# Moving a low part to GpSimd, the last phi(q) forward, and the sixth modulation vector back, in an adaLN block with linear attention and a token-mixing MLP

## The chip, the cores and the metric

One core of a Trainium2 chip runs the kernel. The metric is the device time of one execution in microseconds (us). The core has a matrix engine (PE), a vector engine (VectorE, DVE in the rows), a scalar engine (ScalarE, ACT), a general engine (GpSimd, POOL) and a queue that issues transfers (SyncE, SP). Each of them works through its own list of instructions strictly in order, and waits for the others by semaphores.

## The reference

x has S = 2048 tokens of D = 448 channels, and c is one row that conditions the block. All is float32.

```
mod = (silu(c) @ w_mod) -> sa, ca, ga, sb, cb, gb      # six vectors of D
h = layernorm(x) * (1 + ca) + sa
q, k, v = h @ wqkv                                      # 16 heads of 28
pq, pk = phi(q), phi(k)        # phi(t) = (t + 1 if t > 0 else exp(t)) + 1e-6
kv, z = pk^T v, sum(pk)                                 # per head, over all tokens
o = (pq kv) / (pq z + 1e-6)
x = x + ga * (o @ wo)
h = layernorm(x) * (1 + cb) + sb
u = gelu(h^T @ w1 + b1)                                 # over the token axis, F = 1792
x = x + gb * (u @ w2 + b2)^T
```

The sixth vector of mod, gb, has the index 5 in the kernel.

## The kernel before

The tokens are cut into 16 tiles of 128 (t = 0..15). Every large product is done in the matrix engine's 32-bit rounded format with the operand split in two: a high part (name ending in h) that ScalarE rounds off, and a low part (ending in l), the rest, which is a subtraction. Three products, high x high, high x low and low x high, are added up in one PSUM bank. There are eight banks, and a bank can be given to a new product only when its old contents have been read.

The program is written out in order: the order of the calls in the source is the order in which each engine gets its instructions, and there is no scheduler behind it. Tiles in SBUF come from pools, so that an instruction can also wait for the last reader of a buffer that is used again.

**First stage (0 to about 27 us).** For each token tile, ScalarE makes the high part `hh` of the transposed x, and `a_split_low` makes the low part `hl` on the engine that the tuple `POOL_LOW` names: GpSimd for the tiles in it, VectorE for all others. `projects` multiplies them by the weights into the banks `kp`. Layer norm is applied afterwards: VectorE makes statistics (`a_stats_dve`: `st` on one tile, `mv` and `ve` on a pair), GpSimd raises them to a power (`mv` from `ve` and `roots`), VectorE writes them to `rowst` (`a_rows`), PE transposes that into the bank `rw` (`a_transpose`), ScalarE copies it to the last rows of `hl`, and one more product (L439) closes `kp`. Then ScalarE makes `ek` and `rk` of a closed `kp` (exp and relu) and VectorE makes `pk` of those. The products `cacc` (L550, L554) gather pk^T h.

**Attention and second norm (i = 0..20 of the loop over `NT + LAG`).** Iteration i transposes `pn` of token tile i (bank `tq`, L857), multiplies tile i-1 by the output weights (bank `op`), and runs the first MLP product of tile i-5 for the first four of 14 column groups f (banks `up0` to `up3`, L944 to L946 in `acc3`). The list `late` holds q projections left for this loop; iteration 5 does the last, tile 15. `a_phi_q(nq)` at an iteration's end makes `eq` and `rq` on ScalarE and `pq` on VectorE for all that are projected, but leaves the newest for the next iteration. VectorE has, per iteration, `pd`, `den`, `pn` (attention's division), `x` and `y` (residual and second norm), `ptl` and `pth` (low parts of the transposed tile) and `h2l`, the low part of the MLP's input of which `h2h` is the high part. From iteration 17 on PE also begins the groups 4 to 7 on the first tiles (list `early`, banks `up4` to `up7`).

**The sixth modulation vector.** `mod_part(5, k)`, k = 0..3, adds up four row blocks of w_mod, scaled by silu(c), in `acc5` on VectorE; `mod_add` folds its halves; `mod_high` and its returned function split it into `mh5` on ScalarE and VectorE; `mod_sum2` sums over partitions with one matmul by ones (bank `modp5`, L253); `mod_out` copies the bank to `mod5` on ScalarE (L203), which frees the bank. In the kernel before, the four parts stand in iterations 13 to 16, one each, and the rest in iteration 16. `mod5` is first needed behind the first MLP product, in `finish_u`.

**Second MLP stage (from about 203 us).** The rest of the first MLP product, and then the second one (`y`, L1167 to L1171) by a seven-product scheme.

Of the kernel before, what the change touches and what calls it, by code (L numbers as in the profile page):

```python
# [39 lines left out]
MOD_AT = {11: [(4, 0), (4, 1), (4, 2)], 13: [(4, 3), (4, None), (3, 0), (3, 1)]}  # L40
QS = {0: 3}
WARM = 6
POOL_LOW = (0, 1, 2)
PRE = 9
MID = 5
NSLOT, NTOK = 74, 27
# [5 lines left out]
def block_kernel(ctx: ExitStack, tc: tile.TileContext, x, xt, wqkv, wo, w1, b1, w2, c, wmod, wfirst, out):  # L52
# [26 lines left out]
    def bank(name):  # L79
        return psum.tile([P, 512], F32, name=name, tag="bank")  # L80
# [164 lines left out]
    def mod_split(j):  # L245
        mod_add(j)
        mod_high(j)()
# [125 lines left out]
    def a_stats_dve(ts):  # L373
        g, ve = a_group(ts)

        b6 = {}

        def first(i):
            b6[i] = small.tile([P, 6], F32, name=f"st{ts[i]}", tag="st")
            nc.vector.bn_stats(b6[i], X[ts[i]])  # L380

        def second(i):
            nc.vector.bn_aggr(mv[ts[i]][:, 0:2], b6[i])

        def end():
            nc.vector.tensor_scalar_add(ve, g[:, :, 1:2].to_broadcast([P, len(ts), 2]), EPS)
            a_pow(g, ve)
            groups[ts[0]] = g
        return first, second, end
# [3 lines left out]
    def a_rows(t):  # L393
        g, r = groups.pop(t)[:, :, 0:2], rowst[t // 2 % RING].rearrange("p (t b c) -> p t b c", t=2, b=2)
        nc.vector.tensor_copy(r[:, :, :, 0:2], g.unsqueeze(2).to_broadcast([P, 2, 2, 2]))

        def low():
            nc.vector.tensor_sub(r[:, :, 0, 2:4], g, r[:, :, 0, 0:2].bitcast(F32))
        return low
# [81 lines left out]
    def a_phi_q(keep=0):  # L481
        a_exp_q(keep)
        for t in sorted(eqs):
            pq[t] = phi_q(t)
# [9 lines left out]
    def a_high(t):  # L494
        xss[t] = (slot(f"xh{t}", 512, F32R), slot(f"xl{t}", 384, F32R))
        nc.scalar.activation(xss[t][0][:, :D], xn[t], AF.Copy)
# [127 lines left out]
    a_split_high(6)  # L624
    a_exp(0, kps[0])
    a_high(0)
    low = a_rows(2)
    low()
    a_pk(0, kps[0])
# [1 line left out]
    projects(in_turn(5)[:4], 1, "kp")  # L631
    a_transpose(2)
    projects(in_turn(5)[4:], 1, "kp")
    first45, second45, end45 = a_stats_dve((4, 5))
    first45(0)
    first45(1)
    second45(0)
    second45(1)
# [306 lines left out]
        nc.tensor.matmul(ps[:, :D], hi[:, sl], ml, start=False, stop=False)  # L945
        nc.tensor.matmul(ps[:, :D], lo[:, sl], mh, start=False, stop=last)  # L946

    def step(f0, t, accs, mh, ml):
        k, at = place[f0, t]
        hi, lo = parts[k]  # L950
        for i, ps in enumerate(accs):
            acc3(ps, hi, lo, slice(at + i * P, at + (i + 1) * P), mh, ml, t == 0, t == NT - 1)
        if place.get((f0, t + 1), (0, 0))[0] != k:
            del parts[k]

    a_q(late.pop(0))
# [25 lines left out]
    for i in range(NT + LAG):  # L982
        if i == NT - 4:
            load_mod(5)
        if NT - 3 <= i <= NT:
            mod_part(5, i - NT + 3)
        if i == NT:
            mod_split(5)
        if i % 2 == 0 and 0 < i <= NT:
            b_out_last(i - 2)  # L990
        if i < NT:
            b_transpose(i)
        if 0 <= i - 1 < NT:
            b_out(i - 1)
        nq = min(len(late), QS.get(i, 1))
        for _ in range(nq):
            a_q(late.pop(0))
        t = i - LAG
        if t >= 0:
            if t == 0:  # L1000
                accs = [bank(f"up{f}") for f in range(4)]
            if i > NT:
                if not early:
                    early = [bank(f"up{W1G[1][0] + f}") for f in range(W1G[1][1])]
                r = i - NT - 1
                step(W1G[1][0], r, early, H2h[r], H2l[r])
            step(0, t, accs, H2h[t], H2l[t])
        if i == NT:
            mp = mod_sum2(5)
            mod_out(5, mp)  # L1010
        if i < NT:
            b_high(i)
            if i % 2 == 0:
                b_beside(i)
        a_exp_q(nq)
        scale, res, norm1, norm2 = i + 1 < NT, 0 <= i - 2 < NT, 0 <= i - 3 < NT, 0 <= i - 4 < NT
        if res and i < NT + 1:
            b_res(i - 2)
        if scale:
            b_prod(i + 1)  # L1020
        if norm2:
            b_norm2(i - 4, i)
        if res:
            b_mean1(i - 2, i)
        if norm1:
            b_norm1_a(i - 3)
        if scale:
            b_sum(i + 1)
        if norm1:
            b_norm1_b(i - 3, i)  # L1030
        if scale:
            b_eps(i + 1)
        if i < NT:
            b_low(i)
        if norm1:
            b_mean2(i - 3, i)
        split_end()
        if scale:
            b_recip(i + 1)
        if i < NT:  # L1040
            b_low_last(i)
        if scale:
            b_scale(i + 1)
        if i == NT:
            b_res(i - 1)
        if norm2:
            b_low2(i - 4)
        if i == 1:
            low3()
        if i == 2:  # L1050
            mod_out(3, mod_sum2(3))
        if i == 0:
            for ch in range(4):
                wp_split(ch)
        a_phi_q(nq)
        load_to(max(14 + (i + 1) // 2, 12 + max(0, i - 6) + max(0, i - 14)))
        if res or norm1:
            b_rstd(i, 0 if res else 1, 2 if norm1 else 1)
        split_to(8 + max(0, i - 5))


# [312 lines left out]
```

## Time and profile before

| what | us |
|---|---|
| median of 3 runs | 435.1 (434.35 to 435.51) |
| the profiled execution | 434.17 |
| its span, first to last instruction | 432.5 |
| PE busy | 427.6 (99%) |
| VectorE busy | 364.3 (84%) |
| ScalarE busy | 278.4 (64%) |
| GpSimd busy | 120.6 (28%) |
| granted PE clock | 1.000 |

The 1.7 us between the span and the profiled execution lie around the program and hold no instruction of it. A PE that is busy 99% is not one at its peak: a matmul's row lasts 0.36 us, but the next one starts 0.20 us after it, so that a short wait shows as a larger distance between two starts, even where the rows overlap and PE counts as busy. In a row of the timeline stand the start, the time, the engine, the line, the operation and the tiles written and read; the square brackets tell how long the engine was idle before and what ended that.

### The profile page before, as it was taken

How to read it: one execution, taken by the hardware profiler on the slowest of the kernel's cores; microseconds unless marked ns; L12 is line 12 of the kernel's file. 1: busy time of each engine (PE TensorE's matmuls, PEld its weight loads, DVE VectorE, ACT ScalarE, POOL GpSimd, SP SyncE). 2: the span in 40 equal slices, each digit the busy share in tenths (PEclk: the TensorE clock that was granted, in tenths of full speed). 3: DMA queues.
4: the chain of work that ended last, by engine and by line, in shares of the span. 5: the costliest groups of instructions: out<-in, count | busy, mean ns of one | idle time of the engine just before them, and what ended most of it. 6: DMA issues, size and time to landing. Idle time of an engine off the chain costs nothing.

```text
span 432.5 us, 7208 instructions
## 1 busy us (share of the span) xinstructions
PE 427.6 (99%) x2331; PEld 395.5 (91%) x2331; DVE 364.3 (84%) x814; ACT 278.4 (64%) x595; POOL 120.6 (28%) x199
## 2 busy tenths in 40 slices
PE   8999999999999999999999999999999999999997
PEld 7888899999899989989999999999999999999996
DVE  4999997889899899996579695739798998898894
ACT  5889868657678799985855263537464664655550
POOL 4336444300026577775200000010113131132010
PEclk9999999999999999999999999999999999999999
DMA  8999996564200036345427461577469977885431
GB/s 280 385 316 201 241 262 148 119 196 171 86 1 0 26 74 149 73 107 116 145 85 240 145 212 50 167 205 207 85 186 213 227 161 150 216 181 119 85 46 40
DMA packets 63797, 66.14 MB, mean 153 GB/s; under 512 B 4816, under 2 KB 55312, under 8 KB 63760
## 3 DMA queue, kind: packets, MB, share of 16 engines
q1 hardware_dynamic: 54688, 50.90, 38.1%
q0 software_dynamic: 8784, 14.32, 20.7%
q10 hardware_dynamic: 288, 0.46, 0.4%
q8 instruction: 18, 0.29, 0.3%
q14 instruction: 19, 0.16, 0.1%
HBM read 46.30 MB, written 7.34 MB: 124 GB/s over the span
## 4 chain that ended last, share of the span: by engine, by line
PE 91%; DMA 4%; DVE 3%; ACT 1%; issue 0%; DVEq 0%
PE y L1170 19%; PE up L945 10%; PE up L944 10%; PE up L946 10%; PE y L1171 9%; PE cacc L550 7%; PE qp L432 7%; PE op L887 6%; PE kp L432 5%; DMA xt<-in_xt_dram 2%; DMA wr<-in_qkv_dram 2%; PE tq L857 1%; PE op L894 1%; PE qp L439 1%; PE kvb L812 1%; PE wp L962 1%
## 5 line engine op out<-in xcount | busy, mean ns | idle before, releaser
L945 PE MATMUL up<-h2l,ph 128*128 128x448 f32 x224 | 81.3, 363 | 0.0
L944 PE MATMUL up<-h2h,ph 128*128 128x448 f32 x224 | 81.2, 363 | 0.0
L946 PE MATMUL up<-h2h,pl 128*128 128x448 f32 x224 | 80.8, 361 | 0.0
L1125 POOL DMA_DIRECT2D a<-a x16 | 14.2, 972 | 136.7 <-DMA pr<-in_B_w_dram 75.5
L944 PEld LDWEIGHTS up<-h2h,ph 128*128 128x128 f32 x224 | 42.0, 188 | 3.2
L946 PEld LDWEIGHTS up<-h2h,pl 128*128 128x128 f32 x224 | 41.9, 187 | 3.0
L945 PEld LDWEIGHTS up<-h2l,ph 128*128 128x128 f32 x224 | 42.0, 188 | 2.6 <-DVE h2l L941 0.3
L84 DVE TENSOR_TENSOR pl<-pr,ph 128x512 fp32r<-128x512 f32 x46 | 30.6, 685 | 4.1 <-ACT ph L83 3.3
L1176 ACT ACTIVATE cc<-y 128x448 f32<-128x448 f32 x24 | 13.0, 546 | 26.8 <-PE y L1171 26.8
L83 ACT ACTIVATE ph<-pr 128x512 fp32r<-128x512 f32 x46 | 27.6, 624 | 0.8 <-PE up L946 0.5
L1089 DVE TENSOR_TENSOR u<-u,mod 128x448 f32<-128x448 f32 x14 | 8.7, 621 | 21.7 <-ACT u L1088 21.5
L1190 POOL DMA_DIRECT2D out_dram<-yt x14 | 12.8, 911 | 41.8 <-DVE yt L1181 32.5
L1088 ACT ACTIVATE u<-up,b 128x448 f32<-128x448 f32 x14 | 8.8, 625 | 24.1 <-PE up L946 23.5
L432 PE MATMUL kp<-wh,hh 128*128 128x448 f32 x64 | 23.7, 376 | 0.2 <-ACT rk L449 0.2
L550 PE MATMUL cacc<-pkh,xh 128*128 128x448 f32 x64 | 23.6, 369 | 0.0
L432 PE MATMUL qp<-wh,hh 128*128 128x448 f32 x64 | 23.5, 368 | 0.0
L837 POOL TENSOR_SCALAR den<-den 128x16 f32<-128x16 f32 x16 | 8.8, 550 | 44.7 <-DVE den L834 44.7
L550 PE MATMUL cacc<-pkl,xh 128*128 128x448 f32 x56 | 20.3, 362 | 0.0
L887 PE MATMUL op<-wph,pth 128*128 128x448 f32 x48 | 18.7, 390 | 0.0
L1131 DVE TENSOR_TENSOR a<-a,s 128x512 f32<-128x512 f32 (+1 forms) x32 | 18.4, 616 | 0.0
L83 ACT ACTIVATE s2h<-s 128x512 fp32r<-128x512 f32 (+1 forms) x16 | 8.3, 569 | 15.5 <-DVE s L1131 15.5
L1170 PE MATMUL y<-ub,a11h 128*128 128x448 f32 x56 | 18.2, 375 | 0.0
(235 smaller groups left out, 1379.0 us busy)
## 6 DMA issues: line engine op xcount, KB each, us to landing
pr<-in_B_w_dram SPq DMA_DIRECT2D x56, 256.0 KB, 2.9
a<-in_B_w_dram SPq DMA_DIRECT2D x32, 256.0 KB, 4.6
a<-in_B_w_dram SPq DMA_DIRECT2D x32, 192.0 KB, 4.4
xt<-in_xt_dram SPq DMA_DIRECT2D x16, 256.0 KB, 5.0
x<-in_A_x_dram SPq DMA_DIRECT2D x16, 224.0 KB, 5.0
wm<-in_B_wmod_dram SPq DMA_DIRECT2D x16, 196.0 KB, 5.0
out_dram<-x SPq DMA_DIRECT2D x14, 224.0 KB, 2.4
out_dram<-yt POOLq DMA_DIRECT2D x14, 224.0 KB, 5.3
```

The lines of the kernel that those rows point to most:

```text
L83: nc.scalar.activation(hi, full, AF.Copy)
L84: nc.vector.tensor_sub(lo, full, hi.bitcast(F32))
L432: nc.tensor.matmul(pps[t, j][:, :D], a[:, ch * P:(ch + 1) * P], w, start=first, stop=False)
L550: nc.tensor.matmul(cacc[ch][:, :D], a[:, s], b, start=(t == 0 and i == 0), stop=(t == NT - 1 and i == len(todo) - 1))
L887: nc.tensor.matmul(opb[t][:, :D], a, b, start=(ch == n == 0), stop=False)
L944: nc.tensor.matmul(ps[:, :D], hi[:, sl], mh, start=first, stop=False)
L945: nc.tensor.matmul(ps[:, :D], hi[:, sl], ml, start=False, stop=False)
L946: nc.tensor.matmul(ps[:, :D], lo[:, sl], mh, start=False, stop=last)
L1125: nc.gpsimd.dma_start(w, a, accum_op=ALU.add)
L1131: nc.vector.tensor_tensor(w, raw2[q, a][i], raw2[q, b][i], op=op)
L1170: nc.tensor.matmul(ps[:, :D], h[:, s], w, start=opens and r == 0, stop=False, skip_group_check=True)
L1171: nc.tensor.matmul(ps[:, :HD], l[:, s], wh, start=False, stop=closes and r == PAIRS - 1, skip_group_check=True)
```

## The change

Three things are done in the source.

1. Token tile 5 joins `POOL_LOW`, so that its low part `hl5` is made by GpSimd, and the statistics of the tiles 4 and 5 are begun earlier in the source: `st4` stands before `rowst` of the tiles 2 and 3.
2. `a_phi_q(nq if late else 0)`: in the iteration that has the last q projection, nothing is left for the next iteration.
3. The four `mod_part(5, k)` and `mod_add(5)` stand together at the end of iteration 16, the split of `acc5` in iteration 17, and the matmul `modp5` and the copy `mod5` at the end of iteration 17. `early` gets three banks first; the fourth, `up7`, is taken after `modp5`, and its first tile is multiplied there (`step` gets a `cut` for that).

```diff
-POOL_LOW = (0, 1, 2)
+POOL_LOW = (0, 1, 2, 5)
...
     a_exp(0, kps[0])
     a_high(0)
+    first45, second45, end45 = a_stats_dve((4, 5))
+    first45(0)
     low = a_rows(2)
     low()
     a_pk(0, kps[0])
...
     a_transpose(2)
     projects(in_turn(5)[4:], 1, "kp")
-    first45, second45, end45 = a_stats_dve((4, 5))
-    first45(0)
     first45(1)
...
-    def step(f0, t, accs, mh, ml):
+    def step(f0, t, accs, mh, ml, cut=(0, None)):
         k, at = place[f0, t]
         hi, lo = parts[k]
-        for i, ps in enumerate(accs):
+        for i, ps in list(enumerate(accs))[slice(*cut)]:
             acc3(ps, hi, lo, slice(at + i * P, at + (i + 1) * P), mh, ml, t == 0, t == NT - 1)
-        if place.get((f0, t + 1), (0, 0))[0] != k:
+        if cut[1] is None and place.get((f0, t + 1), (0, 0))[0] != k:
             del parts[k]
...
-        if NT - 3 <= i <= NT:
-            mod_part(5, i - NT + 3)
-        if i == NT:
-            mod_split(5)
...
-                    early = [bank(f"up{W1G[1][0] + f}") for f in range(W1G[1][1])]
+                    early = [bank(f"up{W1G[1][0] + f}") for f in range(W1G[1][1] - 1)]
                 r = i - NT - 1
-                step(W1G[1][0], r, early, H2h[r], H2l[r])
+                step(W1G[1][0], r, early, H2h[r], H2l[r], (0, None if r else 3))
             step(0, t, accs, H2h[t], H2l[t])
-        if i == NT:
-            mp = mod_sum2(5)
-            mod_out(5, mp)
...
+        if i == NT + 1:
+            low5 = mod_high(5)
         if res:
             b_mean1(i - 2, i)
...
+        if i == NT + 1:
+            low5()
         if scale:
             b_eps(i + 1)
...
-        a_phi_q(nq)
+        a_phi_q(nq if late else 0)
...
+        if i == NT:
+            for k in range(4):
+                mod_part(5, k)
+            mod_add(5)
+        if i == NT + 1:
+            mod_out(5, mod_sum2(5))
+            early.append(bank(f"up{W1G[1][0] + 3}"))
+            step(W1G[1][0], 0, early, H2h[0], H2l[0], (3, None))
```

What this does to the order on the engines is shown at three places. A row has the line, the operation and the tiles written and read (the number behind a tile's name is its buffer's), and the shape.

VectorE at 20 to 24 us, in the kernel before, from the variance of the tiles 2 and 3 on:

```order
L415 TENSOR_TENSOR hl4_332<-xt4_153,hh4_331 128x512
L492 TENSOR_SCALAR xn0_357<-x0_135,mv0_282 128x448
L415 TENSOR_TENSOR hl5_346<-xt5_159,hh5_345 128x512
L395 CAST rowst1_103<-mv2_337 128x4x2
L398 TENSOR_TENSOR rowst1_103<-mv2_337,rowst1_103 128x2x2
L454 SCALAR_TENSOR_TENSOR pk0_396<-ek0_387,rk0_388 128x448
L501 TENSOR_TENSOR xh0_391<-xn0_357,xh0_391 128x64
L502 TENSOR_TENSOR xl0_392<-xn0_357,xh0_391 128x384
L380 BN_STATS st4_415<-x4_161 128x6
L380 BN_STATS st5_417<-x5_165 128x6
```

The same place with the change:

```order
L415 TENSOR_TENSOR hl4_332<-xt4_153,hh4_331 128x512
L492 TENSOR_SCALAR xn0_357<-x0_135,mv0_282 128x448
L380 BN_STATS st4_396<-x4_161 128x6
L395 CAST rowst1_103<-mv2_337 128x4x2
L398 TENSOR_TENSOR rowst1_103<-mv2_337,rowst1_103 128x2x2
L454 SCALAR_TENSOR_TENSOR pk0_400<-ek0_387,rk0_388 128x448
L501 TENSOR_TENSOR xh0_391<-xn0_357,xh0_391 128x64
L502 TENSOR_TENSOR xl0_392<-xn0_357,xh0_391 128x384
L380 BN_STATS st5_417<-x5_165 128x6
```

`st4` has taken the place of `hl5`, which has left this engine; on GpSimd it stands between the powers `mv2` and `mv4`.

ScalarE at 139 to 148 us, in the kernel before, from the relu of tile 14 on:

```order
L462 ACTIVATE rq14_1937<-qp14_1831,mv14_989 128x448
L935 ACTIVATE y1_1867<-y1_1867,nb1_1944,rt4_1886 128x448
L938 ACTIVATE h2h1_1947<-y1_1867 128x448
L340 ACTIVATE sqa3_1953,vs5_1952<-x3_157,nm3_1950 128x448
L340 ACTIVATE sqb2_1965,vs5_1952<-y2_1955,ny2_1963 128x448
L865 ACTIVATE pth6_2009<-tq6_1981 128x384
L861 ACTIVATE pn7_2012<-pn6_1970 128x64
L461 ACTIVATE eq15_2014<-qp15_1903,mv14_989 128x448
L462 ACTIVATE rq15_2015<-qp15_1903,mv14_989 128x448
```

The same place with the change:

```order
L462 ACTIVATE rq14_1937<-qp14_1831,mv14_989 128x448
L935 ACTIVATE y1_1867<-y1_1867,nb1_1944,rt4_1886 128x448
L938 ACTIVATE h2h1_1947<-y1_1867 128x448
L340 ACTIVATE sqa3_1953,vs5_1952<-x3_157,nm3_1950 128x448
L340 ACTIVATE sqb2_1965,vs5_1952<-y2_1955,ny2_1963 128x448
L461 ACTIVATE eq15_1973<-qp15_1903,mv14_989 128x448
L462 ACTIVATE rq15_1974<-qp15_1903,mv14_989 128x448
L865 ACTIVATE pth6_2015<-tq6_1987 128x384
L861 ACTIVATE pn7_2018<-pn6_1970 128x64
```

`eq15` and `rq15` have moved ahead of the copy of the transposed tile 6; on VectorE `pq15` moves likewise, from behind `h2l2` to directly behind `pq14`.

VectorE from the end of iteration 16 on, with the change (in the kernel before, the four `acc5` rows stand one each in iterations 13 to 16, and the fold and `mh5` ahead of x14):

```order
L903 SCALAR_TENSOR_TENSOR x15_932,sm15_2782<-op15_2736,x15_932 128x448
L941 TENSOR_TENSOR h2l12_2766<-y12_2711,h2h12_2765 128x448
L230 TENSOR_SCALAR acc5_2793<-wm5_0_2434,sc_194 112x448
L232 SCALAR_TENSOR_TENSOR acc5_2793<-wm5_1_2436,sc_194,acc5_2793 112x448
L232 SCALAR_TENSOR_TENSOR acc5_2793<-wm5_2_2438,sc_194,acc5_2793 112x448
L232 SCALAR_TENSOR_TENSOR acc5_2793<-wm5_3_2440,sc_194,acc5_2793 112x448
L237 TENSOR_TENSOR acc5_2793<-acc5_2793 48x448
L84 TENSOR_TENSOR pl18_2800<-pr18_2274,ph18_2799 128x512
L913 SCALAR_TENSOR_TENSOR y14_2840<-x14_867,nm14_2768,mod4_1477 128x448
L917 SCALAR_TENSOR_TENSOR y14_2840,sy14_2842<-y14_2840,rt16_2791,mod3_1737 128x448
L243 TENSOR_TENSOR mh5_2833<-acc5_2793,mh5_2833 64x448
L941 TENSOR_TENSOR h2l13_2831<-y13_2773,h2h13_2830 128x448
```

Nine rows lie between x15 and `mh5`, of which five make `acc5`.

PE around the matmul `modp5`, in the kernel before:

```order
L946 MATMUL up3_1918<-h2h11_2707,pl11_2281 128x448
L253 MATMUL modp5_2769<-mh5_2740,ones_r_76 128x448
L944 MATMUL up4_2810<-h2h0_1859,ph16_2665 128x448
L945 MATMUL up4_2810<-h2l0_1860,ph16_2665 128x448
L946 MATMUL up4_2810<-h2h0_1859,pl16_2666 128x448
L944 MATMUL up5_2811<-h2h0_1859,ph16_2665 128x448
L945 MATMUL up5_2811<-h2l0_1860,ph16_2665 128x448
L946 MATMUL up5_2811<-h2h0_1859,pl16_2666 128x448
L944 MATMUL up6_2812<-h2h0_1859,ph16_2665 128x448
```

The same matmul with the change:

```order
L946 MATMUL up3_1918<-h2h12_2765,pl12_2355 128x448
L253 MATMUL modp5_2858<-mh5_2833,ones_r_76 128x448
L944 MATMUL up7_2862<-h2h0_1859,ph16_2662 128x448
L945 MATMUL up7_2862<-h2l0_1860,ph16_2662 128x448
L946 MATMUL up7_2862<-h2h0_1859,pl16_2663 128x448
L944 MATMUL up4_2803<-h2h1_1947,ph17_2730 128x448
```

`modp5` stands 21 matmuls later. In the kernel before, `up6` has the bank of `modp5`, with six matmuls between them; with the change `up7` has it, and is the next matmul.

## The prediction

> **What bounds the kernel now.** I read the page first (the chain that ended last, then the chain itself in order of time), then the timeline of each engine where PE's distances show a wait.
>
> ```profile
> span 432.5 us, 7208 instructions
> PE 91%; DMA 4%; DVE 3%; ACT 1%; issue 0%; DVEq 0%
> 57.05 2.00 PE qp L432 x10
> ```
>
> PE sets the end: 91% of the chain is its own queue, and the last row, from the chain, gives its pace, ten matmuls in 2.00 us, 0.20 each. So a change pays only where two of PE's starts lie more than 0.20 apart because an operand or a bank was late, and it costs what it adds to such distances. Stalls removed early are kept, since PE runs at this pace nearly everywhere behind them. The sum below is one of stalls before and after; no matmul is added or removed.
>
> **Part 1, `hl5` on GpSimd, `st4` sooner.**
>
> ```profile
> 21.12 0.68 DVE L415 TENSOR_TENSOR hl<-xt,hh 128x512 fp32r<-128x512 f32 x1
> 21.92 0.16 DVE L398 TENSOR_TENSOR rowst<-mv,rowst 128x4 fp32r<-128x4 f32 x1
> 20.26 1.39 POOL L352 TENSOR_TENSOR mv<-ve,roots 128x4 f32<-128x4 f32 x1 [3.37 <-DVE ve L386]
> L415 POOL TENSOR_TENSOR hl<-xt,hh 128x512 fp32r<-128x512 f32 x3 | 3.9, 1297 | 6.1 <-ACT hh L411 6.1
> 22.35 0.27 PE L404 MATMUL rw<-ident,rowst 128*98 128x128 f32 x1
> 23.07 0.76 PE L432 MATMUL kp<-wh,hl 128*128 128x448 f32 x3
> 22.65 0.57 ACT L407 ACTIVATE hl<-rw 34x128 fp32r<-34x128 f32 x2 [0.84 <-PE rw L404]
> 25.49 0.96 PE L554 MATMUL cacc<-pkl,xh 128*128 128x448 f32 x4
> 26.65 0.29 PE L404 MATMUL rw<-ident,rowst 128*98 128x128 f32 x1 [0.20 <-DVE rowst L398]
> 26.45 0.66 ACT L449 ACTIVATE rk<-kp,mv 128x448 f32<-128x448 f32 x1
> 27.17 0.48 PE L432 MATMUL kp<-wh,hh 128*128 128x448 f32 x1 [0.23 <-ACT rk L449]
> 27.48 0.36 PE L432 MATMUL kp<-wl,hh 128*128 128x448 f32 x1
> ```
>
> GpSimd is free when its power ends at 21.65; `hl5` at 1.30 us (the group of three such rows) ends near 23.0. PE wants it at 23.07, so it comes just in time. VectorE loses one 0.68 row there and puts a 0.62 `st4` in its place, and further on `ve4` and `rowst` of the tiles 4 and 5 come 0.6 sooner. The last of the four L554 matmuls starts near 26.09, so PE could transpose (`rw`) at 26.29 instead of 26.65. That 0.36 us is no gain, though: the next matmul, the first of `kp6`, takes the bank of `kp3` and waits for its last reader, `rk3`, that ends at 27.11, whatever the statistics do. `rk3` stands in an unbroken ScalarE queue that was begun by the copies at 22.65, released by PE's `rw` at 22.35; and PE did not wait there for `rowst`, which was written at 22.08. So **the wait at 27.17 stays**, and this place is worth 0. The same wait covers 0.67 us (26.29 plus 0.20 to 27.17) of a late `hl5`.
>
> What is gained stands later, where VectorE is behind with `hl8`:
>
> ```profile
> 36.75 0.37 PE L432 MATMUL kp<-wl,hh 128*128 128x448 f32 x1
> 37.32 0.36 PE L432 MATMUL kp<-wh,hh 128*128 128x448 f32 x1
> 36.27 0.68 DVE L415 TENSOR_TENSOR hl<-xt,hh 128x512 fp32r<-128x512 f32 x1
> ```
>
> Two steps of PE take 0.57 instead of 0.40, as `hl8` ends at 36.95, when PE was due. VectorE's 0.6 us of relief reaches it unless a wait for ScalarE eats it; I take it: **-0.17 us**, bounds -0.17 and 0.
>
> Can the two engines run side by side there? In the trace VectorE's `hl5` (two operands in SBUF) begins at 21.12, inside GpSimd's power of 20.26 to 21.65, and takes 0.68 like its twins elsewhere; but that power reads a few numbers only. The Trainium skill, page "SBUF — State Buffer", section "Who interferes with whom", says that a VectorE instruction with two inputs in SBUF and a GpSimd instruction that reads SBUF take one read port from each other, and that the later one is blocked for the whole of the earlier; by that the sum would have the price of the third rival. The row of the power does not bear it out, though it is no full test.
>
> **Part 2, the last phi(q) one iteration sooner.**
>
> ```profile
> 144.91 0.49 ACT L865 ACTIVATE pth<-tq 128x384 fp32r<-128x384 f32 x1 [2.49 <-PE tq L857]
> 144.58 0.62 DVE L903 SCALAR_TENSOR_TENSOR x<-op,x 128x448 f32<-128x448 f32 x1 [0.97 <-PE op L894]
> 145.96 0.64 ACT L462 ACTIVATE rq<-qp,mv 128x448 f32<-128x448 f32 x1
> 149.22 0.62 DVE L466 SCALAR_TENSOR_TENSOR pq<-eq,rq 128x448 f32<-128x448 f32 x1
> 149.75 0.62 DVE L903 SCALAR_TENSOR_TENSOR x<-op,x 128x448 f32<-128x448 f32 x1
> 153.94 0.63 DVE L844 SCALAR_TENSOR_TENSOR pn<-pq,den 128x448 f32<-128x448 f32 x1
> 154.17 0.36 PE L894 MATMUL op<-wpl,pth 128*128 128x448 f32 x1
> 154.71 0.52 PE L857 MATMUL tq<-ident,pn 128*128 128x128 f32 x3 [0.19 <-DVE pn L844]
> ```
>
> ScalarE idles 2.49 us before 144.91 and VectorE 0.97 us before 144.58. `eq15` and `rq15` (0.64 each) fit into the first hole, from 142.4 to 143.6, and `pq15` (0.62) into the second, to 144.2. That takes one step of 0.53 us (149.22 to 149.75) out of a VectorE queue that is unbroken from 144.58 to the `pn8` of 153.94, so `pn8` ends at 154.04 instead of 154.57, ahead of the 154.37 at which PE is due: the stall of 0.54 less 0.20 goes, **-0.34 us**. Bounds: -0.34, and 0 if a wait inside that queue takes it up. Cover gone, the price would be the 0.53 back.
>
> **Part 3, the sixth vector.** What it removes: the `acc5` rows, which in iterations 13 to 15 push VectorE's `pn14` and `pn15` behind PE, and the wait in ScalarE's queue for `modp5`.
>
> ```profile
> 184.51 0.36 PE L894 MATMUL op<-wpl,pth 128*128 128x448 f32 x1
> 184.88 0.52 PE L857 MATMUL tq<-ident,pn 128*128 128x128 f32 x3
> 189.64 0.37 PE L946 MATMUL up<-h2h,pl 128*128 128x448 f32 x1
> 190.10 0.63 PE L857 MATMUL tq<-ident,pn 128*128 128x128 f32 x4
> 202.37 0.36 PE L944 MATMUL up<-h2h,ph 128*128 128x448 f32 x1
> 203.00 0.36 PE L946 MATMUL up<-h2h,pl 128*128 128x448 f32 x1
> 197.17 0.36 PE L894 MATMUL op<-wpl,pth 128*128 128x448 f32 x1
> 200.17 0.55 ACT L203 ACTIVATE mod<-modp 128x448 f32<-128x448 f32 x1 [3.53 <-PE modp L253]
> 202.01 0.63 DVE L941 TENSOR_TENSOR h2l<-y,h2h 128x448 fp32r<-128x448 f32 x1 [2.12 <-ACT h2h L938]
> ```
>
> The stalls are 0.37 - 0.20 = 0.17 and 0.46 - 0.20 = 0.26 at the two transposes, and 0.63 - 0.40 = 0.23 at `h2l12`, which was late because ScalarE stood 3.53 us at `mod5` before it made `h2h12`. With the rows gone all three should go: **-0.66 us**; bounds -0.66 and -0.26 (one transpose alone).
>
> What it adds is a new wait on PE. I time it from E, the end of the last matmul of op15 (197.53 in the rows above).
>
> ```profile
> L230 DVE TENSOR_SCALAR acc<-wm,sc 112x448 f32<-112x448 f32 x4 | 1.8, 451 | 0.4 <-PE cacc L550 0.4
> 194.69 0.68 DVE L232 SCALAR_TENSOR_TENSOR acc<-wm,sc,acc 112x448 f32<-112x448 f32 x1
> 195.40 0.62 DVE L237 TENSOR_TENSOR acc<-acc 48x448 f32<-48x448 f32 x1
> 203.84 0.69 DVE L84 TENSOR_TENSOR pl<-pr,ph 128x512 fp32r<-128x512 f32 x1 [1.20 <-ACT ph L83]
> 205.23 0.69 DVE L917 SCALAR_TENSOR_TENSOR y<-y,rt,mod 128x448 f32<-128x448 f32 x1
> ```
>
> VectorE, in its new order: x15 begins about 0.05 behind E (27.11 to 27.17 above is such a step), `h2l12` lasts from E + 0.6 to 1.2, then the first `acc5` row, 0.45 by its group, to 1.6; three more at 0.71 from start to start (194.69 to 195.40), and the fold of 0.62: 4.36. `pl18`, y14 and y14 again stand in between, 1.39 from the start of the first to that of the last (203.84 to 205.23): they begin at 4.39 and 5.78, and the last ends at 6.47. `mh5` follows to **E + 7.0**. PE begins `up` of `h2h11` at E - 0.16 (0.20 behind the row of 197.17) and has 33 matmuls to do, 6.6 us, so `modp5` is due at E + 6.44 and starts at 7.07, 0.06 behind its operand (as 27.11 to 27.17): 0.63 late. Then `up7` needs the bank: 0.36 for `modp5`, 0.04 to ScalarE, 0.55 for `mod5` and 0.06 back, E + 8.08, where it was due at 6.64; and one 0.31 step behind a wait where 0.20 was due (27.17 to 27.48). Together **+1.55 us**. Bounds: the turnaround alone, with `mh5` in time, is 1.01 - 0.20 + 0.11 = 0.92; if `h2h12` comes 0.7 later after E, as GpSimd and ScalarE are placed in the trace, it is 2.2. I take 1.55, because VectorE's chain starts at op15 on PE and moves with PE. Behind PE's wait the whole PE queue stands; ScalarE's `ph19` waits behind `mod5`, but PE needs it only in iteration 20.
>
> The banks are dealt out anew (`up4` and `up6` change places), and loads on SP wait for other buffers' last readers, all of which are read no later than before: 0.
>
> **Sum**: -0.17 - 0.34 - 0.66 + 1.55 = **+0.4 us**, or 434.17 + 0.4 = 434.6 for the profiled execution. That lies 0.9 below the median of 435.1, so the median should be **435.5**: no change, as 0.3%, 1.3 us, is about what a measurement of this kernel can tell from none.
>
> **Rivals.**
>
> *First, only the turnaround is paid.* If the chain on VectorE is shorter than PE's 33 matmuls, 0.92 stands for 1.55: the sum is -0.25, the median 434.9. For it: the chain misses by 0.6 in 7 only. Against: nine rows between x15 and `mh5` are an unbroken dependency of one engine.
>
> *Second, the statistics do pay.* If ScalarE's queue, too, moves up, the stall of 26.29 to 27.17 (0.88, less the transpose's 0.2) and its 0.11 go, 0.8 us: with the first rival -1.05, the median 434.1. Against it stands `rw` at 22.35, which PE reaches by its own queue.
>
> *Third, the two engines shut each other out.* While GpSimd makes `hl5` (21.7 to 23.0), VectorE's two-operand rows wait: `rowst` at 21.92 would run at 23.0, `rw` would start at 23.2 instead of 22.35, and all of ScalarE's queue down to `rk3` and PE's 27.17 would follow by 0.85 to 0.9. VectorE's relief is lost too (0.17). Then 0.4 + 0.17 + 0.9 = +1.45, the median 436.6, slower. It decides from a block of about 0.7 us on. Against: the 0.68 row inside GpSimd's power.
>
> **How the numbers follow.** The forecast 0.60; the first rival 0.20; the second, alone or with the first, 0.08; the third 0.12, since no row here has the two engines both reading whole tiles. Faster by over 0.3% would need the second rival and more: 0.06. Slower takes the third and a late `h2h12`: 0.13. Within: 0.81. The range runs from the second rival's 434.1 to the third's 436.6.
>
> **What would show it.** Right: no wait at 154.7, 184.9 and 190.1; a start of `modp5` late by about 0.6 and `up7` about 1.0 behind it; `kp6` still at 27.2 behind `rk3`. Wrong: `kp6` much before 27 or at 28; `rowst` near 23; `up7` 0.2 behind `modp5`; new waits for `h2l` or for loads behind 205 us.

## The result and the profile after

| what | before | with the change |
|---|---|---|
| median of 6 runs, us | 435.19 (434.35 to 435.51) | 437.58 (436.13 to 437.83) |
| the profiled execution, us | 434.17 | 437.6 |
| its span, us | 432.5 | 435.9 |
| mean granted PE clock of the profiled execution | 1.000 | 0.996 |

The change makes the kernel slower: the ratio is 1.0052, with a 95% interval of 1.0040 to 1.0064, or 2.4 us. The prediction said 435.5 and no more than 436.6. The six runs come in two groups, which matters below: two with a granted clock of 1.0 at 436.13 and 436.19, and four with 0.996 between 437.55 and 437.83. One of 26 executions of the kernel before, on the chip of four of the experiments below, took 1091.37 us and is in no median or ratio here.

Three places of the changed kernel answer to the three parts. The first is the timeline of GpSimd, VectorE, PE and ScalarE at 21 to 29 us (start, time, engine, line, operation, tiles; in brackets the idle time before and what ended it).

```profile
20.41 1.38 POOL L352 TENSOR_TENSOR mv<-ve,roots 128x4 f32<-128x4 f32 x1 [3.37 <-DVE ve L386]
21.76 1.29 POOL L415 TENSOR_TENSOR hl<-xt,hh 128x512 fp32r<-128x512 f32 x1
...
21.82 1.25 DVE L395 CAST rowst<-mv 128x8 fp32r<-128x8 f32 x1
23.11 0.16 DVE L398 TENSOR_TENSOR rowst<-mv,rowst 128x4 fp32r<-128x4 f32 x1
...
23.42 0.29 PE L404 MATMUL rw<-ident,rowst 128*98 128x128 f32 x1 [0.77 <-DVE rowst L398]
28.25 0.48 PE L432 MATMUL kp<-wh,hh 128*128 128x448 f32 x1 [0.60 <-ACT rk L449]
...
27.54 0.66 ACT L449 ACTIVATE rk<-kp,mv 128x448 f32<-128x448 f32 x1
```

GpSimd's `hl5` runs from 21.76 to 23.05, as foreseen. VectorE's CAST of `rowst`, eight numbers to a partition, begins 0.06 behind it and takes 1.25 us; in the kernel before the same row took 0.16:

```profile
21.72 0.16 DVE L395 CAST rowst<-mv 128x8 fp32r<-128x8 f32 x1
```

So `rw` starts at 23.42 instead of 22.35, ScalarE's queue down to `rk3` follows, and `kp6` starts at 28.25 instead of 27.17. Of these 1.08 us, 0.15 stood there before (the last product of line L290 starts at 17.36 instead of 17.21); the rest is the block.

The second is PE at 154.7 us, where the kernel before waited 0.34 us for `pn8`. The step is 0.21 now:

```profile
154.88 0.37 PE L894 MATMUL op<-wpl,pth 128*128 128x448 f32 x1
155.09 0.49 PE L857 MATMUL tq<-ident,pn 128*128 128x128 f32 x3
```

The waits at 184.88, 190.10 and 202.37 are gone too. The third place is the new one, around `modp5`, on PE, VectorE, GpSimd and ScalarE:

```profile
203.67 0.37 PE L946 MATMUL up<-h2h,pl 128*128 128x448 f32 x1
204.70 0.47 PE L253 MATMUL modp<-mh,ones_r 128*128 128x448 f32 x1 [0.67 <-DVE mh L243]
206.14 0.47 PE L944 MATMUL up<-h2h,ph 128*128 128x448 f32 x1 [0.97 <-ACT mod L203]
...
204.03 0.62 DVE L243 TENSOR_TENSOR mh<-acc,mh 64x448 fp32r<-64x448 f32 x1
...
204.08 0.64 POOL L922 TENSOR_SCALAR ny<-sy 128x1 f32<-128x1 f32 x1 [2.17 <-DVE y L917]
...
204.75 0.67 ACT L340 ACTIVATE sqb<-y,ny 128x448 f32<-128x448 f32 x1 [0.93 <-POOL ny L922]
205.54 0.54 ACT L203 ACTIVATE mod<-modp 128x448 f32<-128x448 f32 x1
```

`modp5` is 0.83 late (due at 203.87), and `up7` starts 1.43 behind it. What follows was in no step of the prediction. The windows of the changed kernel (stretch, its length, busy time and number of instructions of PE, of its weight loads, of VectorE, ScalarE and GpSimd, then the granted clock, the share of the DMA engines and GB/s):

```profile
200.32:203.74 3.42, 3.42 (x19) 3.14 (x17) 3.15 (x6) 2.38 (x5) 1.51 (x3) 1.00 0.39 69
203.74:207.15 3.41, 1.78 (x8) 1.15 (x7) 2.02 (x5) 1.91 (x5) 2.03 (x4) 1.00 0.46 148
207.15:210.56 3.41, 3.41 (x11) 3.01 (x10) 2.09 (x5) 2.35 (x5) 1.10 (x3) 0.50 0.29 82
210.56:213.98 3.42, 3.42 (x18) 3.21 (x18) 1.62 (x3) 2.58 (x5) 0.89 (x3) 1.00 0.58 192
```

Behind PE's two waits, from 207.15 on, the clock was granted at 0.50 for 3.41 us. PE got 11 matmuls done there instead of 18; they start 0.37 apart, not 0.20.

### The profile page after: what moved, and what is told of

Its sections match the earlier page's. It is cut to its first block, busy times and chain, and to the rows that moved or that the text cites. A ratio compares the mean times of both kernels' runs of the same rounds, so it can differ in the third digit from the quotient of the medians.

```text
span 435.9 us, 7215 instructions
## 1 busy us (share of the span) xinstructions
PE 428.7 (98%) x2331; PEld 397.3 (91%) x2331; DVE 365.5 (84%) x813; ACT 278.8 (64%) x595; POOL 122.9 (28%) x200
## 4 chain that ended last, share of the span: by engine, by line
PE 91%; DVE 3%; DMA 2%; ACT 1%; issue 1%; POOL 0%; SPq 0%; DVEq 0%
PE y L1175 19%; PE up L946 10%; PE up L944 10%; PE up L945 10%; PE y L1176 9%; PE cacc L550 7%; PE qp L432 7%; PE op L887 7%; PE kp L432 5%; PE op L894 1%; PE tq L857 1%; DMA wt<-in_first_dram 1%; DMA wr<-in_qkv_dram 1%; PE qp L439 1%; PE kvb L812 1%; PE wp L962 1%
## 5 line engine op out<-in xcount | busy, mean ns | idle before, releaser
L946 PE MATMUL up<-h2h,pl 128*128 128x448 f32 x224 | 81.9, 366 | 0.0
```

## The experiments

Three causes were on the table. **Theory X**: GpSimd's `hl5` shuts VectorE's CAST out (the prediction's third rival, on another row than it named). **Theory Q**: `up7` comes 1.43 behind `modp5` because the square `sqb14` stands in front of the copy `mod5` on ScalarE. **Theory C**: PE's two waits, both within about 3.4 us, lower its clock for the stretch behind; against it **theory D**, that the clock fell for a reason outside part 3.

A run's time wanders by about 1 us in all of these kernels (434.06 to 435.40 in 25 runs of the kernel before on one chip), and in the profiles the wandering lies in the first 18 us: the last product for `rowb` (L290) in the first stage starts at 17.20 in one kernel and 18.26 in another, before any edit takes effect. So beside each median stands what the profiles show from that row on, in three stretches that do not hold the wandering: A from that L290 to the first `kp6`, B from there to the first L290 of the next weights (49.38 in the kernel before), C from there to PE's end. The kernel before has 9.95, 22.21 and 380.07 us. The differences, in us:

| kernel | A | B | C | sum | median against before (95%) | runs with a fallen clock |
|---|---|---|---|---|---|---|
| the change | +0.95 | -0.34 | +2.67 | +3.3 | +2.4 (+1.7 to +2.8) | 4 of 6 |
| part 1 alone | +0.93 | -0.35 | -0.01 | +0.6 | +0.8 (+0.3 to +1.1) | 0 of 11 |
| `hl5` on GpSimd alone | +0.84 | +0.10 | -0.03 | +0.9 | +1.1 (+0.5 to +1.3) | 0 of 11 |
| half of `hl5` on GpSimd | +0.40 | +0.11 | +0.03 | +0.5 | +0.9 (+0.3 to +1.0) | 0 of 11 |
| part 2 alone | 0.00 | +0.02 | -0.34 | -0.3 | -0.5 (-0.9 to -0.1) | 0 of 11 |
| part 3 alone | 0.00 | -0.01 | +3.09 | +3.1 | +2.8 (+1.9 to +2.9) | 4 of 5 |
| parts 2 and 3 | 0.00 | +0.03 | +1.19 | +1.2 | +1.8 (+1.0 to +2.3) | 4 of 9 |
| the change, 4 matmuls more | +0.94 | -0.35 | +1.08 | +1.7 | +1.5 (+0.9 to +1.9) | 0 of 7 |
| the change, 2 matmuls more | +0.93 | -0.37 | +1.08 | +1.6 | +1.2 (+0.9 to +2.1) | 0 of 5 |
| parts 2 and 3, copy first | +0.01 | -0.01 | +0.87 | +0.9 | +0.5 (+0.3 to +1.0) | 0 of 11 |
| parts 2 and 3, late bank | 0.00 | -0.01 | -1.05 | -1.1 | -1.3 (-1.7 to -0.8) | 0 of 7 |

The differences of medians are worked out from the runs on the same chip, their intervals from those of the ratios. The profiled executions of the change and of part 3 are ones with a fallen clock, those of all others not. The change's sum is above its difference of medians because its profiled execution, 437.6, lies at its median, and that of the kernel before, 434.17, below all six of its runs.

### Part 1 alone

```diff
-POOL_LOW = (0, 1, 2)
+POOL_LOW = (0, 1, 2, 5)
...
+    first45, second45, end45 = a_stats_dve((4, 5))
+    first45(0)
     low = a_rows(2)
     low()
...
-    first45, second45, end45 = a_stats_dve((4, 5))
-    first45(0)
```

> The kernel before with part 1 alone (hl5 on GpSimd, the first rows of the statistics sooner). Theory X (GpSimd's hl5 and VectorE's CAST behind it shut each other out): CAST rowst starts near 21.8 and takes about 1.25 us instead of 0.16, rw starts near 23.4 instead of 22.35, the first kp6 near 28.1 to 28.3 instead of 27.17; the stall at hl8 goes (-0.17). Net about +0.8 to +0.9 us, and a granted clock of 1.0 to the end. Theory Y (the lateness at rw in the changed kernel belongs to its run, not to part 1): kp6 at 27.2, about -0.17 us.

The ratio is 1.0016 (1.0007 to 1.0025), +0.79 us by the medians. The timeline of VectorE, GpSimd and PE:

```profile
21.66 1.25 DVE L395 CAST rowst<-mv 128x8 fp32r<-128x8 f32 x1
...
21.60 1.28 POOL L415 TENSOR_TENSOR hl<-xt,hh 128x512 fp32r<-128x512 f32 x1
...
28.08 0.47 PE L432 MATMUL kp<-wh,hh 128*128 128x448 f32 x1 [0.60 <-ACT rk L449]
```

The CAST ends at 22.91, 0.03 behind GpSimd's row, and A is longer by 0.93. So the delay belongs to part 1, and theory Y falls. What part 1 was to win, it wins: B is shorter by 0.35. That is twice the 0.17 of the prediction, since with `hl8` two more short waits of PE go (steps of 0.31 at 34.02 and 0.28 at 41.65 in the kernel before).

### Only `hl5` on GpSimd

The statistics stay at their old place.

```diff
-POOL_LOW = (0, 1, 2)
+POOL_LOW = (0, 1, 2, 5)
```

> The kernel before with hl5 on GpSimd alone; the first rows of the statistics stay at their old place. Theory X: the same as part 1, CAST about 1.25 us, rw near 23.3, kp6 0.9 late; net +0.7 us. Rival Z (the earlier st4 is what pushes VectorE's CAST behind GpSimd's start): without st4 ahead of it the CAST starts before GpSimd's hl5, takes 0.16, rw at 22.4, and kp6 stays at about 27.2: -0.17 us.

The ratio is 1.0021 (1.0012 to 1.0030), +1.13 us. VectorE and GpSimd in its timeline:

```profile
21.64 0.51 DVE L492 TENSOR_SCALAR xn<-x,mv 128x448 f32<-128x448 f32 x1
22.62 1.25 DVE L395 CAST rowst<-mv 128x8 fp32r<-128x8 f32 x1 [0.48 <-POOL mv L352]
...
22.56 1.28 POOL L415 TENSOR_TENSOR hl<-xt,hh 128x512 fp32r<-128x512 f32 x1
```

Rival Z falls. VectorE stands idle for 0.48 us ahead of the CAST, which cannot start sooner as it reads what GpSimd's power writes; and GpSimd starts `hl5` as soon as its power ends, a moment before VectorE has seen that end. The order of the statistics has no part in it. It has one in the gain: without the sooner statistics B is 0.10 longer, not 0.35 shorter, so the waits around `hl8` stay.

### Half of `hl5` on GpSimd

The kernel before, with `hl5` in two halves of 256 columns, the first on VectorE, the second on GpSimd.

```diff
-        eng = nc.gpsimd if t in POOL_LOW else nc.vector
-        eng.tensor_sub(heads[t][1], XT[t], heads[t][0].bitcast(F32))
+        for eng, c in HALVES if t == 5 else [(nc.gpsimd if t in POOL_LOW else nc.vector, slice(0, 512))]:
+            eng.tensor_sub(heads[t][1][:, c], XT[t][:, c], heads[t][0][:, c].bitcast(F32))
         XT[t] = None
+    HALVES = [(nc.vector, slice(0, 256)), (nc.gpsimd, slice(256, 512))]
```

> The kernel before, with hl5 made in two halves of 256 columns: the first on VectorE at its old place, the second on GpSimd; the statistics stay where they were. Theory X (VectorE's CAST is shut out for as long as GpSimd's instruction lasts): GpSimd's half takes about 0.65 us from 21.6 on, the CAST rowst takes about 0.6 instead of 0.16, rw starts at about 22.7, and the first kp6 is 0.3 late, not 0.9; about +0.2 us with half of the stall at hl8 gone. Rival Y (the CAST is late by a fixed amount as soon as GpSimd has a second row behind its power): CAST 1.25, rw at 23.3, kp6 0.9 late.

VectorE, GpSimd and PE in its timeline:

```profile
22.16 0.70 DVE L395 CAST rowst<-mv 128x8 fp32r<-128x8 f32 x1
22.90 0.17 DVE L398 TENSOR_TENSOR rowst<-mv,rowst 128x4 fp32r<-128x4 f32 x1
...
22.10 0.74 POOL L415 TENSOR_TENSOR hl<-xt,hh 128x256 fp32r<-128x256 f32 x1
...
23.21 0.29 PE L404 MATMUL rw<-ident,rowst 128*98 128x128 f32 x1 [0.23 <-DVE rowst L398]
```

GpSimd's row is 0.74 long, and the CAST 0.70, ending 0.02 behind it: the block is as long as GpSimd's instruction, and rival Y falls. A is 0.40 longer (0.3 was expected). The relief behind, half of the wait at `hl8`, which was expected too, did not come: B is 0.11 longer. The median, +0.86 us with an interval from +0.3 to +1.0, is above the sum of 0.54, but does not tell it from 0.54.

### Part 2 alone

```diff
-        a_phi_q(nq)
+        a_phi_q(nq if late else 0)
```

> The kernel before with part 2 alone (the last phi(q) an iteration sooner). The prediction's step: the stall of 154.71 goes, -0.34 us, and nothing comes in its place. Rival: VectorE or ScalarE is late elsewhere for it, 0 or up to +0.2 us. Granted clock 1.0 in both.

C is 0.34 shorter, to the hundredth what was predicted, and nothing takes the place of the wait. The ratio is 0.9989 (0.9980 to 0.9998).

### Part 3 alone, and parts 2 and 3

The edits are those of the change with the lines of the other parts left as they were.

> The kernel before with part 3 alone (the sixth modulation vector behind iteration 16). Removed: the stalls at 184.9, 190.1 and 202.4, -0.66 us. Added, as the changed kernel's trace has it: modp5 0.83 late, up7 1.43 behind it, 0.11 for the restart, less 0.20 that was due, +2.17. So +1.5 us while the clock holds. Theory C (PE's two waits just ahead lower its clock for one stretch of about 3.4 us): in part of the runs the granted clock falls to 0.5 near 207 to 211, mean clock .996, and the time is another 1.7 us longer, +3.2 in those runs. Theory D (the clock fell in the changed kernel for a reason outside part 3): clock 1.0 in all runs, +1.5 us.

> The changed kernel without its part 1 (parts 2 and 3 alone). If the parts add up: the changed kernel less part 1's +0.8 to +0.9 us, so about +1.2 us against the kernel before while the clock holds, and about 1.7 more in runs in which it falls. Theory C expects that fall in some runs here too, at another share of them, since PE reaches the place about 1.1 us sooner; theory D (part 1's shift is what makes it fall) expects clock 1.0 in all.

Part 3 alone: 1.0055 (1.0043 to 1.0067). The windows of its profile, of which PE's waits lie in the first:

```profile
203.35:206.76 3.41, 1.78 (x8) 1.08 (x7) 2.02 (x5) 2.10 (x6) 1.85 (x4) 1.00 0.45 119
206.76:210.18 3.42, 3.42 (x11) 3.02 (x10) 2.31 (x6) 2.62 (x5) 1.03 (x4) 0.50 0.37 111
```

Parts 2 and 3: 1.0038 (1.0024 to 1.0053); PE in the profiled execution, whose clock did not fall:

```profile
203.12 0.37 PE L946 MATMUL up<-h2h,pl 128*128 128x448 f32 x1
204.27 0.47 PE L253 MATMUL modp<-mh,ones_r 128*128 128x448 f32 x1 [0.78 <-DVE mh L243]
205.70 0.48 PE L944 MATMUL up<-h2h,ph 128*128 128x448 f32 x1 [0.96 <-ACT mod L203]
```

Theory D falls: part 3 alone lowers the clock in four of five runs, and parts 1 and 2 in none of eleven each. But the same two waits, 0.95 and 1.23 us here, do not lower it in every run: four of nine with parts 2 and 3. The clock records that the trace of the changed kernel and that of part 3 hold show why this may be (start and length in us, granted share):

```
the change:  5.765 201.386 1.0   207.151 3.413 0.5   210.564 225.280 1.0
part 3:      5.376 201.386 1.0   206.763 3.413 0.5   210.176 225.280 1.0
```

All lengths are whole numbers of 3.413 us (59, 1, 66): the clock is set on a grid with that step, and the grid starts at another time in each run. In these two profiles one step, 203.74 to 207.15 and 203.35 to 206.76, holds the whole of both waits. Counting as waiting the time from 0.20 behind the last start before a wait to the next start, that step has 0.83 + 1.24 = 2.07 us of it in the change, and 0.83 + 1.23 = 2.06 in part 3. Where a border of the grid cuts the waits, each of two steps has less. That this is what spares the other runs stays an inference: the profile of parts 2 and 3 holds no clock record, so its grid is not known. The next section has a further hint.

### More work ahead of `modp5`

The changed kernel with FILL matmuls, 4 or 2, into `modp5`'s bank just ahead of `modp5`, which then writes over their result.

```diff
-    def mod_sum2(j):
-        ps = bank(f"modp{j}")
+    def mod_sum2(j, ps=None):
+        ps = ps or bank(f"modp{j}")
...
         if i == NT + 1:
-            mod_out(5, mod_sum2(5))
+            fill = bank("modp5")
+            for m in range(FILL):
+                nc.tensor.matmul(fill[:, :D], parts[done["split"] - 1][0][:, :P], H2h[0], start=True, stop=True)
+            mod_out(5, mod_sum2(5, fill))
```

> The changed kernel with four matmuls more, whose result is thrown away, in modp5's bank just ahead of modp5, so that PE works for about 0.8 us more of the stretch in which it otherwise waits for mh5. Theory C (the clock falls where one window of 3.41 us holds about 2 us of waiting): the waiting in such a window falls to about 1.3 us, the clock stays at 1.0 in all runs, up7 still 1.43 behind modp5, and the time is that of the changed kernel's runs without the fall, +1.0 to +1.4 us against the kernel before. Rival (it is up7's wait behind modp5 alone, 1.23 us with nothing running, that lowers the clock): it falls in most runs still, +2.4 us.

> The changed kernel with two matmuls more ahead of modp5 (result thrown away), where four kept the clock at 1.0 in all runs: about 1.65 us of waiting within one window of 3.41 us, between the 1.25 of four and the 2.05 of none. If the fall hangs on the waiting within one window, it comes in none or in fewer than the changed kernel's runs (four of six); the time is that of the four, +1.5 us, while the clock holds, and 1.7 more in runs where it falls. If instead any work ahead of modp5 had kept the clock (the stretch without work cut in two), no run falls.

With four: 1.0032 (1.0021 to 1.0043), with two: 1.0035 (1.0021 to 1.0048), and the clock is 1.0 in all twelve runs. Work that nobody needs makes the kernel faster than in the runs in which the clock falls: C is 1.6 us shorter than in the profile of the change (+1.08 against +2.67), although `modp5` and `up7` start no sooner. That is the price of the fall, and the rival by which `up7`'s wait alone would bring it is gone, since that wait is as long as before. The step of the grid that holds PE's waits, of the kernel with four, of that with two, and of the next section's:

```profile
203.86:207.27 3.41, 2.45 (x12) 1.83 (x11) 2.02 (x5) 1.89 (x5) 2.05 (x4) 1.00 0.47 133
```

```profile
202.58:205.99 3.41, 2.24 (x10) 1.50 (x8) 2.48 (x5) 2.46 (x8) 1.03 (x3) 1.00 0.27 77
```

```profile
203.36:206.77 3.41, 2.00 (x9) 1.59 (x9) 1.70 (x5) 1.71 (x4) 1.36 (x3) 1.00 0.48 148
```

PE was busy there for 2.45, 2.24 and 2.00 us, and the clock held; in the change and in part 3 it was busy for 1.78, and the clock fell. The kernel with two matmuls does not tell whether less waiting or any work between the waits kept the clock, as both expect 1.0; the next section's does, which has no work there and only less waiting.

The end of the profiles has more such steps, since PE stops some 3 us ahead of the span's end. The first is of the kernel with the copy first, the second of the one with half of `hl5` on GpSimd:

```profile
428.64:432.05 3.41, 1.81 (x17) 1.63 (x15) 1.31 (x4) 0.00 (x0) 0.00 (x0) 1.00 0.20 68
428.88:432.30 3.42, 1.58 (x15) 1.40 (x13) 1.12 (x3) 0.00 (x0) 0.00 (x0) 1.00 0.20 67
```

Behind the first the clock record holds 1.0 for one more step, behind the second it has 0.5 from 432.30 on. So in these profiles the border lies between 1.78 and 1.81 us of busy time in a step, or about 1.6 us without a matmul, and one stretch without work does as much as two waits. Matmul ends are modelled, so its last digit is not certain. An estimate from it: the two waits of the change leave PE empty for 0.67 + 0.97 = 1.64 us, so the clock falls only where one step holds nearly all of both. With four matmuls they leave 0.96, with two 0.27 + 0.96 = 1.23, with the copy first 0.78 + 0.63 = 1.41, all below 1.6 wherever the grid lies. That agrees with the absence of a fall in the 23 runs of these three kernels.

### The copy `mod5` ahead of `sqb14`

Parts 2 and 3, with the matmul and the copy written ahead of iteration 17's square.

```diff
         if i == NT + 1:
             low5()
+            mod_out(5, mod_sum2(5))
...
         if i == NT + 1:
-            mod_out(5, mod_sum2(5))
             early.append(bank(f"up{W1G[1][0] + 3}"))
```

> Parts 2 and 3 without part 1, with one row moved on ScalarE: mod5's copy stands ahead of the square sqb14 instead of behind it. Theory Q (up7 is 1.43 behind modp5 and not 1.01 because sqb14, itself held by GpSimd's ny14 of 0.64 us instead of 0.21, stands in front of the copy): the copy starts about 0.5 behind modp5's start, up7 about 1.1 behind it, 0.3 us less than in parts 2 and 3 alone while the clock holds; by the rows +0.85 us against the kernel before. Rival (the restart behind modp5 costs 1.43 whatever ScalarE has queued): up7 1.43 behind still. For the clock: about 1.85 us of waiting in one window instead of 2.2; it falls in as many or fewer runs.

The ratio is 1.0015 (1.0006 to 1.0023). PE and ScalarE in its timeline:

```profile
204.19 0.47 PE L253 MATMUL modp<-mh,ones_r 128*128 128x448 f32 x1 [0.78 <-DVE mh L243]
205.29 0.47 PE L944 MATMUL up<-h2h,ph 128*128 128x448 f32 x1 [0.63 <-ACT mod L203]
...
204.69 0.54 ACT L203 ACTIVATE mod<-modp 128x448 f32<-128x448 f32 x1 [1.38 <-PE modp L253]
205.13 0.66 ACT L340 ACTIVATE sqb<-y,ny 128x448 f32<-128x448 f32 x1
```

`up7` is 1.10 behind `modp5`, and C is 0.32 shorter than with parts 2 and 3 as they were (0.87 against 1.19). Theory Q holds; the chain of the prediction (matmul, copy, restart) gives 0.47 + 0.03 + 0.54 + 0.06 once nothing stands in between. In none of eleven runs did the clock fall.

### A later place for `modp5` and `up7`

Parts 2 and 3, with `modp5` behind the second tile of `up4` to `up6`, and the first two tiles of `up7` behind the twelve matmuls of `up0` to `up3` that follow.

```diff
-                step(W1G[1][0], r, early, H2h[r], H2l[r], (0, None if r else 3))
+                step(W1G[1][0], r, early, H2h[r], H2l[r], (0, None if r > 1 else 3))
+            if i == NT + 2:
+                mp = mod_sum2(5)
             step(0, t, accs, H2h[t], H2l[t])
+            if i == NT + 2:
+                mod_out(5, mp)
...
-        if i == NT + 1:
-            mod_out(5, mod_sum2(5))
+        if i == NT + 2:
             early.append(bank(f"up{W1G[1][0] + 3}"))
-            step(W1G[1][0], 0, early, H2h[0], H2l[0], (3, None))
+            for r in range(2):
+                step(W1G[1][0], r, early, H2h[r], H2l[r], (3, None))
```

> Parts 2 and 3 without part 1, but with modp5 nine matmuls later (behind the second tile of up4 to up6), and the first two tiles of up7 behind the twelve matmuls of up0 to up3 that follow it, so that mod5's copy is hidden. Theory (part 3 costs only its two waits, and the clock only because of them): no wait at modp5 (due about 205.3, mh5 ready at 204.2) nor at up7 (due about 207.7, mod5 copied by 206.4), clock 1.0 in all runs, and the gains of parts 2 and 3 remain: -0.34 - 0.66 = -1.0 us, 433.8 against a median of 434.8. Rival (VectorE's and ScalarE's rows of the sixth vector are late for the tiles behind it, or PE waits for h2l13): gaps of PE behind 205, -0.5 us or less.

The ratio is 0.9971 (0.9960 to 0.9982): 433.34 us against 434.62 on the same chip, faster than the kernel before by 1.3 us and so than the change by some 3.7. PE and ScalarE, and the windows:

```profile
205.18 0.36 PE L253 MATMUL modp<-mh,ones_r 128*128 128x448 f32 x1
205.38 0.36 PE L944 MATMUL up<-h2h,ph 128*128 128x448 f32 x1
...
207.78 0.36 PE L944 MATMUL up<-h2h,ph 128*128 128x448 f32 x1
...
205.70 0.55 ACT L203 ACTIVATE mod<-modp 128x448 f32<-128x448 f32 x1
```

```profile
203.74:207.15 3.41, 3.41 (x18) 3.20 (x18) 2.51 (x5) 2.45 (x5) 1.72 (x4) 1.00 0.48 144
207.15:210.56 3.41, 3.41 (x18) 3.20 (x18) 1.96 (x4) 2.34 (x6) 1.27 (x4) 1.00 0.46 144
```

No wait is left: `modp5` follows its neighbour by 0.20, and `up7` at 207.78 finds its bank read since 206.25. C is 1.05 shorter: this is what parts 2 and 3 remove when they add nothing, -1.00 in the prediction.

## Why the prediction was wrong, point by point

By the rows of the profiles the change costs 3.3 us, not 0.4. Three steps make up the difference: a block between GpSimd and VectorE that was put at nothing (0.95), new waits of PE that were sized too small (0.62), and a fall of the clock that no step had (1.6); against them the gains were 0.2 larger than planned. It is the clock that took the time out of the range: the two runs in which the clock held, 436.13 and 436.19, lie inside it, above the 435.5 that was forecast.

**Part 1, the engines side by side: wrong, and the mechanism that was set aside is the one that came.** The signs of being wrong that the prediction named, `kp6` at 28 and `rowst` near 23, are in the trace (28.25 and 23.11). The prediction weighed the block and set it aside with "The row of the power does not bear it out, though it is no full test", and named as evidence "the 0.68 row inside GpSimd's power". That row was read too quickly. Here are the VectorE row under which that power starts, the next pair of the same kind, and the power of 24.79 itself, all of the kernel before:

```profile
20.09 0.68 DVE L415 TENSOR_TENSOR hl<-xt,hh 128x512 fp32r<-128x512 f32 x1
...
24.62 0.62 DVE L521 SCALAR_TENSOR_TENSOR pkl<-pk,pkh 128x448 fp32r<-128x448 f32 x1
...
24.79 1.31 POOL L352 TENSOR_TENSOR mv<-ve,roots 128x4 f32<-128x4 f32 x1 [3.14 <-DVE ve L386]
```

The power of 20.26 starts under a VectorE row with two operands in SBUF that ends at 20.77, and takes 1.39; the power of 24.79 starts under such a row that ends at 25.24, and takes 1.31. Less the overlap, 0.51 and 0.45, both last 0.88 and 0.86. So the row that was taken as evidence against the block can be read as an instance of it, with GpSimd as the engine that waits; that the second `hl` of VectorE was not delayed fits if the power had by then read its few numbers. The eight powers of the kernel before agree with it: the one of 56.53, which starts under a row that reads a bank (`wrow`, L295), takes 1.03, the seven others 1.17 to 1.69. This reading was not tried by a run of its own. The block by rows of `hl5` was: 1.25 under 1.28 and 0.70 under 0.74. The Trainium skill, page "SBUF — State Buffer", section "Who interferes with whom", says that a VectorE instruction with two inputs in SBUF contends with GpSimd, that a cast can too, by a mode that uses both of VectorE's ports, and that the later one is blocked for the whole of the earlier. The CAST's times agree with that, down to 0.02 us. The third rival priced it well (+0.85 to +0.9 at `kp6`; 0.93 to 0.95 was measured), but on the row behind the CAST, L398, which ran in 0.16, and with a loss of VectorE's relief that did not come.

The kernel before also had rows that bear the block out. L908 and L922 are the same GpSimd operation on one number to a partition, and its time depends on VectorE's row beside it:

```profile
133.64 0.68 DVE L913 SCALAR_TENSOR_TENSOR y<-x,nm,mod 128x448 f32<-128x448 f32 x1
135.36 0.55 DVE L872 TENSOR_TENSOR ptl<-tq,pth 128x384 fp32r<-128x384 f32 x1
...
133.74 0.66 POOL L908 TENSOR_SCALAR nm<-sm 128x1 f32<-128x1 f32 x1
135.65 0.23 POOL L922 TENSOR_SCALAR ny<-sy 128x1 f32<-128x1 f32 x1
```

VectorE's row for `y` reads two tiles in SBUF, the one for `ptl` reads one of its two from the bank `tq`. Of the 32 GpSimd rows of these lines, the 14 that start under a VectorE row with two tiles in SBUF take 0.53 to 0.66 us, and the 18 others 0.21 to 0.23. Nor is it true that "no row here has the two engines both reading whole tiles": VectorE's rows for `wt` (L224), at 6.15 and 6.70, run beside GpSimd's first `hl` (5.68, 1.27 us). They take their usual 0.62, and one of their operands, `scr`, is in a bank.

**Part 1, the wait at 27.17 and `hl8`: mostly right.** `kp6` hangs on `rk3`, and `rk3` on `rw`; this is why a late CAST reaches PE at all. The term of -0.17 measured -0.35. Its reason, "VectorE's 0.6 us of relief reaches it", was incomplete: with `hl5` gone and the statistics at their old place the waits stayed.

**Part 2: right**, -0.34 against -0.34.

**Part 3, what it removes: right.** With part 2, -1.00 was predicted and -1.05 measured, in the kernel with the late bank.

**Part 3, what it adds: the mechanism right, the size too small.** "**+1.55 us**" measured 2.17 in the change: `modp5` 0.83 late instead of 0.63, `up7` 1.43 behind it instead of 1.01, and the restart of 0.11. The 0.2 of the first come from VectorE's rows from `pl18` to `mh5`, which the prediction packed closer than they ran (`mh5` starts at 204.03, 6.60 behind the end of op15, instead of 6.4). Of the 0.42 of the second, 0.33 is the step "0.04 to ScalarE", which took 0.37: the copy stood behind `sqb14`, as the experiment with the copy first shows. The rest is the matmul behind a wait, which lasts 0.47, not 0.36. `sqb14` was late because `ny14` on GpSimd took 0.64 instead of its usual 0.21. It starts at 204.08 under VectorE's `mh5` (two operands in SBUF, until 204.65): one more row of the kind above, though no run has `ny14` alone. The bound of 2.2 was met by luck: its reason was a late `h2h12`, and `h2l12` starts at 198.02, 0.6 behind the end of op15 as planned.

**The clock: not in the prediction, and the step that failed by most.** "The sum below is one of stalls before and after" takes PE's pace between the stalls, 0.20 a matmul, as given. Behind the two new waits the pace itself was 0.37 for 3.41 us, at a granted clock of 0.50. No term, no rival and no bound of the range had this, although the granted clock stood in the table of the profile before. It costs 1.6 us in four of six runs, and by itself moves the median from about 436.2 to 437.6. The prediction's sum with the measured sizes, without the clock, is -0.35 + 0.95 - 1.05 + 2.17 = +1.7 us, as in the two kernels with more matmuls. Their ratios of 1.0032 and 1.0035 say that the change would be slower without the fall, too, but only by about as much as the range allowed.

## What to carry to other kernels

Before a row is moved to GpSimd, list what VectorE starts while it runs, small casts too, and price each row with two operands in SBUF, and each cast, as blocked until GpSimd's row ends; where GpSimd has just written what VectorE waits for, the two start together. For the rows with two operands this is the cautious price: in these runs it was the cast that waited. A new wait on PE has a second price where it comes on top of another: add up the time in which PE has no matmul in each stretch of 3.4 us, and where it comes near the 1.6 us of this case, put independent matmuls between the waits or shorten one of them. A row whose time is longer than that of its twins belongs with the row of the other engine that it overlaps, before it is used as evidence for anything.

## What the runs showed of the hardware that was not expected

PE's granted clock fell to 0.50 for one step of 3.413 us behind a step in which PE was busy for 1.78 us (2.06 to 2.07 of waiting), and held with 1.81, 2.00, 2.24 and 2.45 us busy. The mean granted clock shows a fall in 12 of the 20 runs of the three kernels with part 3's waits in full and in none of the 30 runs of the four in which they were shortened, filled or removed. The Trainium skill, page "TensorE: Matmul & The Clock Gate", section "Part 1: The HAM clock gate (the "warmup" mystery)", tells of such a window of 3413 ns that runs freely, and of half clock behind an idle one. The length and the half agree. The trace differs in what counts as idle: around `modp5` no wait was longer than 1.24 us, and a step in which PE worked for half the time was enough.

A cast of 128 by 8 numbers took 1.25 us instead of 0.16 beside a GpSimd subtraction, and GpSimd rows of one number to a partition 0.53 to 0.71 instead of 0.21 to 0.23 under a VectorE row with two tiles in SBUF. Neither shows as a wait in the brackets of the timeline: a blocked row only looks long.
